# Attention and a gated unit on one core: K and Q in tiles of their own, small VectorE operations moved to ScalarE or PSUM

## The chip, the cores and the metric

The kernel runs on one core of a Trainium2 chip. The core has TensorE (PE in the profile; its weight loads are PEld), VectorE (DVE), ScalarE (ACT), GpSimd (POOL) and SyncE (SP), which here only issues the DMAs. Each engine works through a queue of its own in order; they meet through semaphores. SBUF is the working memory, PSUM holds TensorE's results in eight banks. The metric is the device time of one execution in microseconds; of the kernel before it is 1375.41 us, the median of 3 runs (1374.64 to 1376.36).

## The reference

Attention with queries that are averaged in pairs, and then a gated unit with a spatial product. All is float32 outside; two of the weights come as float64.

```python
# attention: B=8, H=8, S=1152, D=64
q_pool = q.reshape(B, H, S // 2, 2, D).mean(axis=3)          # 576 queries
scores = scale * np.matmul(q_pool, k.transpose(0, 1, 3, 2))  # 576 x 1152
attn = softmax(scores)                                       # with the row maximum taken away
x = (attn @ v) with the heads side by side                   # 8 x 576 x 512
# gated unit: w_in 512 x 1024, w_spatial 576 x 576, w_out 512 x 512
h = np.maximum(x @ w_in, 0.0)
u, v = h[..., :512], h[..., 512:]
v_n = (v - mean(v)) / np.sqrt(var(v) + 1e-06)
v_s = np.einsum('ts,bsd->btd', w_spatial, v_n) + b_spatial[None, :, None]
out = (u * v_s) @ w_out
```

## The kernel before

**Pairs and units.** The 64 heads are worked off as 32 pairs of one batch (`i` from 0 to 31). Two batches, so eight pairs, make one unit of the gated part; there are four units. Products are made with float16 or bfloat16 pieces of each operand, a high and a low part, so one float32 product is three matmuls.

**One pair.** `load_kq` (L218) fetches K and Q of the pair into one tile `kq`, K first, 576 KB each; the tile exists once. `prep` (L273) forms the squares' sums of K and Q on ScalarE (`square_sum`, L132), sums them over the partitions with a matmul of ones (L112), and makes of the sum's exponent a power of two for scaling, `s`, and its inverse, `r` (`scales`, L107: three VectorE operations L117, L121, L122 on a tile of two columns, with `h` = `qkh`, `s` = `qks`, `r` = `qkr`). The product of both `r` is `esc` (L287), the scale of the exponential. GpSimd adds Q's two halves (L292). Then the high parts come from ScalarE (L135 for Q, L302 and L304 for K) and the low parts from VectorE for Q (`rest`, L138) and from GpSimd for K (L305). Copies of halves across partitions go through DMAs (L299 to L313). `maxima` (L317) makes each query's maximum: 27 products per pair into `pm` banks and a maximum by VectorE for each (L348). `attention` (L498) makes the scores (L506, L507, bank `pss`), the exponential on ScalarE (L512, tile `pt`, and L520 for the tail), splits it on GpSimd (L524), and multiplies it with the values (L428, L432, L435, bank `o`).

**Beside the attention.** While pair `i` is worked on, `maxima` of pair `i + 1`, the values of the next ones (L229, L261 to L264) and `prep` of pair `i + 2` are mixed in at set rates, in the early pairs the decoding of the float64 weights (`from_double`, L144: masks, shifts and products on VectorE with L150 and L157 on ScalarE), and later a step of the gated unit (`gated_unit`, L546) at every second turn. In the unit, the first products give `vv` (L582, L590), statistics follow (L592, L593), four Newton steps for the inverse root (L611 to L614, on 9 columns), the normalised values (L618 to L624), the other half `u` (L646, L656), the spatial product (L688, L689, in two `pw` banks), bias and gate (L695 to L698), and the last product (L731). The last unit's later parts run after the last pair. The factors `r_h` (L568, L570), `r_v` (L635) and `r_y` (L707) are columns that scale a product back.

**What sets the order.** The source says what depends on what and in which order it is written; a scheduler then places the instructions in each engine's queue by its own estimate of when each can start, and adds the semaphores. So an edit at one place moves instructions at many others. PSUM is shared out by pools: 3 banks `pss`, 2 banks `pm` (maxima, the sums of `scales`, transposes), 1 bank `o`, 2 banks `pw` (the gated unit). A bank is given to the next user when the last instruction on its tile is done.

Of the kernel before, what the change touches and what calls it, by code (L numbers as in the profile page):

```python
# [12 lines left out]
F32 = mybir.dt.float32  # L13
I32 = mybir.dt.int32
I64 = mybir.dt.int64
AF = mybir.ActivationFunctionType
ALU = mybir.AluOpType
# [7 lines left out]
SVN = 2.0 ** 11  # L25
# [6 lines left out]
def attn_sgu_kernel(ctx: ExitStack, tc: tile.TileContext, qT, kT, v, w_in, w_spT, b_sp, w_out, out):  # L32
    nc = tc.nc
    P = 128
# [3 lines left out]
    KEYS = NC * P  # L38
# [67 lines left out]

    def scales(sq, name):  # L107


        n = sq.shape[1]  # L110
        pt = ps_m.tile([P, 512], F32, name="pm")
        nc.tensor.matmul(pt[:, :n], lhsT=ones, rhs=sq, start=True, stop=True)  # L112
        yield
        h = sm.tile([P, n], I32, name=name + "h", bufs=2)
        s = sm.tile([P, n], I32, name=name + "s", bufs=2)
        r = sm.tile([P, n], I32, name=name + "r", bufs=2)
        nc.vector.tensor_scalar(  # L117
            out=h, in0=pt[:, :n].bitcast(I32), scalar1=24, scalar2=0x7F, op0=ALU.logical_shift_right, op1=ALU.bitwise_and
        )
        c = float(2 ** 23)  # L120
        nc.vector.tensor_scalar(out=s, in0=h, scalar1=-c, scalar2=204 * c, op0=ALU.mult, op1=ALU.add)  # L121
        nc.vector.tensor_scalar(out=r, in0=h, scalar1=c, scalar2=50 * c, op0=ALU.mult, op1=ALU.add)  # L122
        return s.bitcast(F32), r.bitcast(F32)
# [7 lines left out]
    def square_sum(acc, src, junk):  # L131
        nc.scalar.activation(junk, src, AF.Square, bias=0.0, scale=1.0, accum_out=acc)  # L132

# [10 lines left out]
    def from_double(dst, src, t1, t2):  # L144


        V = nc.vector
        lo, hi = src[:, 0::2], src[:, 1::2]
        V.tensor_scalar(out=t1, in0=hi, scalar1=0xFFFFF, scalar2=None, op0=ALU.bitwise_and)
        nc.scalar.activation(dst, t1, AF.Copy, bias=1.0, scale=2.0 ** -20)  # L150
        V.tensor_scalar(out=t2, in0=lo, scalar1=1, scalar2=None, op0=ALU.logical_shift_right)
        yield
        V.scalar_tensor_tensor(out=dst, in0=t2, scalar=2.0 ** -51, in1=dst, op0=ALU.mult, op1=ALU.add)
        yield
# [9 lines left out]
    wsc = {}  # L164
# [53 lines left out]
    def load_kq(i):  # L218

        b, hp = divmod(i, NHP)  # L220
        kq = ld.tile([P, 2 * KEYS], F32, name="kq")
        nc.sync.dma_start(out=kq[:, 0:KEYS], in_=kT[b, hp].rearrange("h d c p -> (h d) (c p)"))
        nc.sync.dma_start(out=kq[:, KEYS:], in_=qT[b, hp].rearrange("h d r s -> (h d) (r s)"))
        state[i] = {"kq": kq}

# [47 lines left out]
    def prep(i):  # L273
        st = state[i]
        kq = st["kq"]
        X, KL, khh, qhl = (x[i % NSET] for x in (xq, klo, khi, qhi))
        k0 = kq[:, 0:KEYS].rearrange("p (c k) -> p c k", k=P)
        q0, q1 = kq[:, KEYS : KEYS + S], kq[:, KEYS + S :]
# [8 lines left out]
        nc.vector.scalar_tensor_tensor(  # L287
            out=esc, in0=r[:, 0:1], scalar=ESC, in1=r[:, 1:2], op0=ALU.mult, op1=ALU.mult
        )
        st["esc"] = esc  # L290
# [255 lines left out]
    def gated_unit(un):  # L546
# [20 lines left out]
        for e in range(2):  # L567
            nc.vector.tensor_mul(r_h[:, e : e + 1], vscale[2 * un + e][1], wsc["wi"])  # L568
# [40 lines left out]
        for k in range(4):  # L609
            z = SVN if k == 3 else 1.0  # L610
            nc.vector.tensor_mul(sd, rs, rs)  # L611
            nc.vector.tensor_mul(sd, sd, va)
            nc.vector.tensor_scalar(out=sd, in0=sd, scalar1=-0.5 * z, scalar2=1.5 * z, op0=ALU.mult, op1=ALU.add)
            nc.vector.tensor_mul(rs, rs, sd)  # L614
# [56 lines left out]
        def spatial(e, fc):  # L671
# [22 lines left out]
            for a, n, pz, ba in ((m0, MAIN, pv, 0), (tl0, TAIL, pvt, MAIN)):  # L694
                nc.vector.scalar_tensor_tensor(  # L695
                    out=gg[:, :n], in0=pz[:, :n], scalar=r_v, in1=b_bc[:, ba : ba + n], op0=ALU.mult, op1=ALU.add
                )
                nc.vector.tensor_mul(u[:, fc, a : a + n], u[:, fc, a : a + n], gg[:, :n])  # L698
            k = 2 * fc + e
# [3 lines left out]
        def split(n):  # L703
            a, z = groups[n]
            s_g, r_g = yield from scale_of(gsq[:, 2 * a : 2 * z], "g")
            r_y = sm.tile([P, 1], F32, name=f"r_y{n}")
            nc.vector.tensor_mul(r_y, r_g, wsc["wo"])  # L707
            if n == 0:
# [174 lines left out]
```

## Time and profile before

| | before |
|---|---|
| time, median of 3 runs | 1375.41 us (1374.64 to 1376.36) |
| the profiled execution | 1378.83 us, span 1377.1 us |
| mean granted TensorE clock | 0.967 |
| busy: TensorE, VectorE, ScalarE, GpSimd | 89%, 70%, 70%, 62% |
| bytes moved by DMAs | 123.77 MB |

A line of the groups is: source line, engine, operation, tiles written and read, shapes, count, then the busy time of the group in us with the mean of one in ns, and the idle time of the engine just before the group with what ended it. A line of the waits is: who waited, for whom, us in total, how often, the longest. A line of the windows is: from, to and length of the stretch, then for PE, PEld, DVE, ACT and POOL the busy time and the number of instructions, the granted clock, the DMA engines' share, GB/s; asked of one source line, it has that line's engine alone. A line of the order of time is: start, length, engine, line, operation, tiles, and in brackets the idle time before it. An instruction that has begun and waits inside the engine counts as busy.

### The profile page before, as it was taken

The numbers are of one execution on the slowest core, as the hardware profiler recorded it, in microseconds if no ns is written. First come the engines' busy times: TensorE is split into PE (matmuls) and PEld (weight loads), VectorE is DVE, ScalarE is ACT, GpSimd is POOL, SyncE is SP. The second block draws the span as 40 slices with busy tenths as digits, with TensorE's granted clock in tenths as the row PEclk, the third lists the DMA queues.
The fourth block names the chain that finished last, engine by engine and source line by source line (L and its number), as shares of the span: only waits on it lengthen the run. The fifth ranks groups of instructions, "written<-read, shape, count | busy, mean of one in ns | idle before, by whom it ended". The sixth has DMA issues, their size and how long they took to land.

```text
span 1377.1 us, 33478 instructions
## 1 busy us (share of the span) xinstructions
PE 1222.1 (89%) x13696; PEld 741.5 (54%) x13696; DVE 967.1 (70%) x2068; ACT 970.6 (70%) x1632; POOL 847.0 (62%) x492
## 2 busy tenths in 40 slices
PE   3677887788998999889998999889998999899998
PEld 1354555555554665556555666555555566556443
DVE  5799889986869767765668766775667866761455
ACT  6777678779966777768776886768776776655333
POOL 3587677878755666657774766667666576655000
PEclk9998899989999999999999999999999999999999
DMA  7533343434333231244332132244331131101002
GB/s 252 166 97 109 94 124 94 128 93 139 113 96 96 79 94 56 62 126 135 96 96 87 51 91 84 74 118 135 104 96 42 47 94 55 28 24 40 8 1 69
DMA packets 56346, 123.77 MB, mean 90 GB/s; under 512 B 8256, under 2 KB 16448, under 8 KB 56192
## 3 DMA queue, kind: packets, MB, share of 16 engines
q1 hardware_dynamic: 56192, 121.63, 29.8%
q8 instruction: 107, 1.75, 0.5%
q14 instruction: 47, 0.39, 0.1%
HBM read 83.56 MB, written 9.44 MB: 68 GB/s over the span
## 4 chain that ended last, share of the span: by engine, by line
PE 47%; DVE 25%; ACT 8%; POOL 7%; DMA 7%; issue 4%; SPq 1%; POOLq 0%; ACTq 0%; DVEq 0%
DVE mt L348 7%; PE pss L507 5%; PE pss L506 5%; PE pw L688 5%; POOL pt L524 4%; PE pm L342 4%; PE pw L731 4%; PE pw L646 3%; PE o L435 3%; PE o L428 3%; PE pw L582 3%; ACT pt L512 3%; DMA kq<-in_qT_dram 3%; PE o L432 3%; DVE vv L138 2%
## 5 line engine op out<-in xcount | busy, mean ns | idle before, releaser
L524 POOL TENSOR_TENSOR pt<-pt 128x1024 f16<-128x1024 f32 x288 | 567.8, 1977 | 265.9 <-ACT pt L512 253.8
L512 ACT ACTIVATE pt<-pss,lnp,esc 128x512 f32<-128x512 f32 x576 | 439.4, 776 | 156.7 <-PE pss L507 148.1
L348 DVE TENSOR_REDUCE mt<-pm 128x1 f32<-128x384 f32 x730 | 395.8, 552 | 139.1 <-PE pm L342 119.2
L435 PE MATMUL o<-vp,pt 128*128 128x65 f16 x2304 | 282.8, 198 | 20.2 <-POOL pt L524 19.9
L428 PE MATMUL o<-vp,pt 128*128 128x65 f16 x2304 | 284.8, 196 | 13.0 <-DVE xm L443 12.8
L506 PE MATMUL pss<-qhi,khi 128*128 128x64 f16 (+1 forms) x1152 | 279.6, 294 | 9.1 <-ACT pt L512 8.0
L432 PE MATMUL o<-vp,pt 128*128 128x64 f16 x2304 | 284.5, 196 | 0.0
L507 PE MATMUL pss<-xq,klo 66*128 66x64 f16 (+1 forms) x1152 | 280.6, 295 | 4.1 <-DMA xq<-mr 4.1
L428 PEld LDWEIGHTS <-pt 128*128 128x128 bf16 x2304 | 222.7, 101 | 85.1 <-DVE xm L443 22.0
L432 PEld LDWEIGHTS <-pt 128*128 128x128 bf16 x2304 | 221.6, 100 | 50.7 <-issue 10.5
L342 PE MATMUL pm<-khi,qhi 128*128 128x384 f16 x652 | 217.9, 335 | 32.6 <-DVE mt L348 27.7
L435 PEld LDWEIGHTS <-pt 128*128 128x128 f16 x2304 | 220.7, 100 | 31.6 <-POOL pt L524 24.8
L507 PEld LDWEIGHTS <-klo 66*128 66x128 f16 x1152 | 99.1, 100 | 48.8 <-issue 17.3
L132 ACT ACTIVATE klo<-kq 128x1152 f16<-128x1152 f32 x64 | 74.6, 1166 | 63.7 <-DMA kq<-in_kT_dram 49.4
L506 PEld LDWEIGHTS <-khi 128*128 128x128 f16 x1152 | 103.5, 100 | 27.9 <-issue 12.2
L342 PEld LDWEIGHTS <-qhi 128*128 128x128 f16 x768 | 76.8, 101 | 66.3 <-issue 28.5
L524 POOL TENSOR_TENSOR ptl<-ptl 128x1152 f16<-128x1152 f32 x32 | 71.1, 2221 | 57.9 <-ACT ptl L520 57.9
L305 POOL TENSOR_TENSOR klo<-kq,khi 128x640 f16<-128x640 f32 x64 | 85.1, 1341 | 20.1 <-ACT khi L304 19.8
L520 ACT ACTIVATE ptl<-pss,lnp,esc 128x256 f32<-128x256 f32 (+1 forms) x128 | 75.6, 591 | 24.8 <-PE pss L507 24.2
L264 POOL TENSOR_TENSOR vp<-vt,vp 128x576 f16<-128x576 f32 x64 | 80.6, 1264 | 20.3 <-ACT vp L262 20.3
L582 PE MATMUL pw<-wi_h,xg 128*128 128x512 f16 x240 | 90.1, 382 | 0.0
L731 PE MATMUL pw<-wo_h,vv 128*128 128x512 f16 x216 | 80.3, 381 | 4.7 <-DVE vv L138 4.7
(177 smaller groups left out, 2394.2 us busy)
## 6 DMA issues: line engine op xcount, KB each, us to landing
vt<-in_v_dram SPq DMA_DIRECT2D x64, 576.0 KB
kq<-in_kT_dram SPq DMA_DIRECT2D x32, 576.0 KB
kq<-in_qT_dram SPq DMA_DIRECT2D x32, 576.0 KB
khi<-khi SPq DMA_DIRECT2D x96, 144.0 KB
out_dram<-row SPq DMA_DIRECT2D x24, 256.0 KB
qhi<-xq SPq DMA_DIRECT2D x64, 72.0 KB
klo<-klo SPq DMA_DIRECT2D x32, 144.0 KB
vv<-in_w_in_dram SPq DMA_DIRECT2D x8, 512.0 KB
```

What stands on the lines that cost most here:

```text
L305: nc.gpsimd.tensor_sub(KL[:, 0, a:z], k0[:, a:z], khh[:, 1, a:z])
L342: nc.tensor.matmul(pm[:, :W], lhsT=qhl[:, h, c0 : c0 + P], rhs=khh[:, h, n * NB : (n + 1) * NB, :], start=True, stop=True,)
L348: nc.vector.reduce_max(out=mt[:, t, n : n + 1], in_=pm[:, :W], axis=AX.X)
L428: nc.tensor.matmul(o[:, t], lhsT=top[:, cols], rhs=vp[:, D : D + D1], start=c == 0 and t == 0, stop=False, skip_group_check=True,)
L432: nc.tensor.matmul(o[:, t, 0:D], lhsT=top[:, cols], rhs=vp[:, 0:D], start=False, stop=False, skip_group_check=True)
L435: nc.tensor.matmul(o[:, t], lhsT=rst[:, cols], rhs=vp[:, D : D + D1], start=False, stop=c == NC - 1, skip_group_check=True,)
L506: nc.tensor.matmul(o, lhsT=khh[:, h, c, :], rhs=qhl[:, h, q], start=True, stop=False)
L507: nc.tensor.matmul(o, lhsT=KL[0:KR, h, c, :], rhs=X[0:KR, h, q], start=False, stop=True)
L512: nc.scalar.activation(pt, ps, AF.Exp, bias=lnp, scale=esc)
L524: nc.gpsimd.tensor_sub(t.bitcast(F16)[:, :, 0::2], t, t.bitcast(BF16)[:, :, 1::2])
L582: nc.tensor.matmul(ph, lhsT=xa[:, cc, c0 : c0 + P], rhs=wa[:, cc, DH:DF], start=n == 0, stop=n == 3 * NCC - 1,)
L731: nc.tensor.matmul(py, lhsT=ga[:, fc, c0 : c0 + P], rhs=wa[:, fc, :], start=m == 0, stop=m == end - 1)
```

## The change

- K and Q get tiles of their own, `kt` (one buffer) and `qt` (two); Q is fetched first, and Q's sum of squares is formed before K's.
- `scales` keeps `h` in the PSUM bank of the sum, in columns beside it; `r` is made before `s`, and both have four buffers. The constant in `esc` moves into `r` for K and Q, as half its logarithm each.
- `esc`, `r_h`, `r_v` and `r_y` are made on ScalarE, as a copy with a column as scale; `r_h`'s third column comes straight from its factors, without the copy L570.
- `from_double` no longer shifts the low words by one bit (L151); the product L153 reads them as unsigned numbers with half the factor.
- In the Newton steps `va` and `sd` lie in a `pm` bank, and the products are formed in another order, so that each has one operand in PSUM and one in SBUF.
- The bias (L695) is written back to the `pw` bank, and the gate's product (L698) reads it there.

```diff
-    def scales(sq, name):
+    def scales(sq, name, up=0):
...
-        h = sm.tile([P, n], I32, name=name + "h", bufs=2)
-        s = sm.tile([P, n], I32, name=name + "s", bufs=2)
-        r = sm.tile([P, n], I32, name=name + "r", bufs=2)
+        h = pt[:, 16 : 16 + n].bitcast(I32)
+        s = sm.tile([P, n], I32, name=name + "s", bufs=4)
...
+        r = sm.tile([P, n], I32, name=name + "r", bufs=4)
+        nc.vector.tensor_scalar(out=r, in0=h, scalar1=c, scalar2=(50 + up) * c, op0=ALU.mult, op1=ALU.add)
         nc.vector.tensor_scalar(out=s, in0=h, scalar1=-c, scalar2=204 * c, op0=ALU.mult, op1=ALU.add)
-        nc.vector.tensor_scalar(out=r, in0=h, scalar1=c, scalar2=50 * c, op0=ALU.mult, op1=ALU.add)
...
-        lo, hi = src[:, 0::2], src[:, 1::2]
+        lo, hi = src.bitcast(U32)[:, 0::2], src[:, 1::2]
...
-        V.tensor_scalar(out=t2, in0=lo, scalar1=1, scalar2=None, op0=ALU.logical_shift_right)
-        yield
-        V.scalar_tensor_tensor(out=dst, in0=t2, scalar=2.0 ** -51, in1=dst, op0=ALU.mult, op1=ALU.add)
+        yield
+        V.scalar_tensor_tensor(out=dst, in0=lo, scalar=2.0 ** -52, in1=dst, op0=ALU.mult, op1=ALU.add)
...
-        kq = ld.tile([P, 2 * KEYS], F32, name="kq")
-        nc.sync.dma_start(out=kq[:, 0:KEYS], in_=kT[b, hp].rearrange("h d c p -> (h d) (c p)"))
-        nc.sync.dma_start(out=kq[:, KEYS:], in_=qT[b, hp].rearrange("h d r s -> (h d) (r s)"))
+        kt = ld.tile([P, KEYS], F32, name="kt")
+        qt = ld.tile([P, KEYS], F32, name="qt", bufs=2)
+        nc.sync.dma_start(out=qt, in_=qT[b, hp].rearrange("h d r s -> (h d) (r s)"))
+        nc.sync.dma_start(out=kt, in_=kT[b, hp].rearrange("h d c p -> (h d) (c p)"))
...
-        for j in range(2):
-            square_sum(sq[:, j : j + 1], kq[:, j * KEYS : (j + 1) * KEYS], KL[:, 0].rearrange("p c k -> p (c k)"))
+        for j, t in ((1, qt), (0, kt)):
+            square_sum(sq[:, j : j + 1], t, KL[:, 0].rearrange("p c k -> p (c k)"))
             yield
-        s, r = yield from scales(sq, "qk")
+        s, r = yield from scales(sq, "qk", math.log2(ESC) / 2)
         esc = sm.tile([P, 1], F32, name="esc", bufs=NSET)
-        nc.vector.scalar_tensor_tensor(
-            out=esc, in0=r[:, 0:1], scalar=ESC, in1=r[:, 1:2], op0=ALU.mult, op1=ALU.mult
-        )
+        nc.scalar.activation(esc, r[:, 0:1], AF.Copy, bias=0.0, scale=r[:, 1:2])
...
-            nc.vector.tensor_mul(r_h[:, e : e + 1], vscale[2 * un + e][1], wsc["wi"])
             rows = slice(e * TAIL, (e + 1) * TAIL)
-            nc.vector.tensor_copy(out=r_h[rows, 2:3], in_=r_h[rows, e : e + 1])
+            r_x = vscale[2 * un + e][1]
+            nc.scalar.activation(r_h[:, e : e + 1], r_x, AF.Copy, bias=0.0, scale=wsc["wi"])
+            nc.scalar.activation(r_h[rows, 2:3], r_x[rows], AF.Copy, bias=0.0, scale=wsc["wi"][rows])
...
-        va = sm.tile([P, NT], F32, name="va")
-        sd = sm.tile([P, NT], F32, name="sd")
+        pt = ps_m.tile([P, 512], F32, name="pm")
+        va, sd = (pt[:, 16 * k : 16 * k + NT] for k in range(2))
...
-            nc.vector.tensor_mul(sd, rs, rs)
-            nc.vector.tensor_mul(sd, sd, va)
+            nc.vector.tensor_mul(sd, rs, va)
+            nc.vector.tensor_mul(sd, rs, sd)
...
-        nc.vector.tensor_scalar_mul(r_v, wsc["ws"], 1.0 / SVN)
+        nc.scalar.activation(r_v, wsc["ws"], AF.Copy, bias=0.0, scale=1.0 / SVN)
...
-                    out=gg[:, :n], in0=pz[:, :n], scalar=r_v, in1=b_bc[:, ba : ba + n], op0=ALU.mult, op1=ALU.add
+                    out=pz[:, :n], in0=pz[:, :n], scalar=r_v, in1=b_bc[:, ba : ba + n], op0=ALU.mult, op1=ALU.add
                 )
-                nc.vector.tensor_mul(u[:, fc, a : a + n], u[:, fc, a : a + n], gg[:, :n])
+                nc.vector.tensor_mul(u[:, fc, a : a + n], u[:, fc, a : a + n], pz[:, :n])
...
-            nc.vector.tensor_mul(r_y, r_g, wsc["wo"])
+            nc.scalar.activation(r_y, r_g, AF.Copy, bias=0.0, scale=wsc["wo"])
```

The scheduler places the instructions anew, and the line numbers of the changed kernel are up to two higher. Three places of the queues follow. The first is SyncE's queue in one pair, in the stage with the gated unit; L222 and L223 fetch K and Q, L299 to L313 are the copies of `prep`, L363 those of the maxima, L741 stores the result. Before:

```order
L300 DMA qhi_120<-qhi_120 64x576
L307 DMA khi_117<-khi_117 64x1152
L308 DMA khi_117<-khi_117 64x1152
L309 DMA qhi_120<-xq_114 64x576
L312 DMA klo_108<-klo_108 64x1152
L222 DMA kq<-in_kT_dram 128x1152
L310 DMA khi_117<-khi_117 64x1152
L741 DMA out_dram<-row 128x512
L363 DMA xq_113<-mr 1x9x128 x2
L313 DMA klo_108<-klo_108 2x1152
L223 DMA kq<-in_qT_dram 128x1152
```

And of the changed kernel (L224 fetches Q, L225 fetches K):

```order
L300 DMA qhi_120<-qhi_120 64x576
L224 DMA qt<-in_qT_dram 128x1152
L309 DMA qhi_120<-xq_114 64x576
L307 DMA khi_117<-khi_117 64x1152
L308 DMA khi_117<-khi_117 64x1152
L312 DMA klo_108<-klo_108 64x1152
L225 DMA kt<-in_kT_dram 128x1152
```

K's fetch keeps its place behind the copy of K's low part (L312); Q's stood behind K's with four rows between, and stands ahead of it now with four rows between.

The second is VectorE's queue where the scales of a pair and of the first weight are made, in the early stage (`wih`, `wis`, `wir` are the weight's; L443 and L402 are the attention's output). Before:

```order
L117 TENSOR_SCALAR qkh<-pm 128x2
L117 TENSOR_SCALAR wih<-pm 128x1
L121 TENSOR_SCALAR qks<-qkh 128x2
L122 TENSOR_SCALAR qkr<-qkh 128x2
L121 TENSOR_SCALAR wis<-wih 128x1
L122 TENSOR_SCALAR wir<-wih 128x1
L287 SCALAR_TENSOR_TENSOR esc<-qkr 128x1
L348 TENSOR_REDUCE mt<-pw 128x1
L568 TENSOR_TENSOR r_h<-vr,wir 128x1 x2
L570 COPY r_h<-r_h 64x1 x2
L402 TENSOR_TENSOR xg<-pm,xg 128x512
```

And of the changed kernel:

```order
L118 TENSOR_SCALAR pm<-pm 128x2
L118 TENSOR_SCALAR pm<-pm 128x1
L151 TENSOR_SCALAR vv<-vv 128x512
L123 TENSOR_SCALAR qkr<-pm 128x2
L124 TENSOR_SCALAR qks<-pm 128x2
L123 TENSOR_SCALAR wir<-pm 128x1
L124 TENSOR_SCALAR wis<-pm 128x1
L402 TENSOR_TENSOR xg<-pm,xg 128x512
```

`esc` and `r_h` have left the queue, and the scales read the bank `pm`; a mask of the decoding (L151 there, L149 before) stands between.

The third is VectorE's queue at a gate of the first unit, between the maxima. Before:

```order
L695 SCALAR_TENSOR_TENSOR row<-pw,r_v,b_bc 128x512
L348 TENSOR_REDUCE mt<-pm 128x1 x2
L698 TENSOR_TENSOR u<-u,row 128x512
L348 TENSOR_REDUCE mt<-pm 128x1
L695 SCALAR_TENSOR_TENSOR row<-pw,r_v,b_bc 128x64
L348 TENSOR_REDUCE mt<-pm 128x1
L698 TENSOR_TENSOR u<-u,row 128x64
```

And of the changed kernel:

```order
L696 SCALAR_TENSOR_TENSOR pw<-pw,r_v,b_bc 128x512
L348 TENSOR_REDUCE mt<-pm 128x1 x3
L699 TENSOR_TENSOR u<-u,pw 128x512
L696 SCALAR_TENSOR_TENSOR pw<-pw,r_v,b_bc 128x64
L348 TENSOR_REDUCE mt<-pm 128x1
L699 TENSOR_TENSOR u<-u,pw 128x64
```

Three maxima stand between the bias and the gate now, and the bank `pw` is in use until the second of the two.

More of the change, by code (lines that the diff above doesn't have):

```diff
@@ L15 @@
 I64 = mybir.dt.int64
+U32 = mybir.dt.uint32
 AF = mybir.ActivationFunctionType
@@ L220, in load_kq @@
         b, hp = divmod(i, NHP)
-        kq = ld.tile([P, 2 * KEYS], F32, name="kq")
-        nc.sync.dma_start(out=kq[:, 0:KEYS], in_=kT[b, hp].rearrange("h d c p -> (h d) (c p)"))
-        nc.sync.dma_start(out=kq[:, KEYS:], in_=qT[b, hp].rearrange("h d r s -> (h d) (r s)"))
-        state[i] = {"kq": kq}
+        kt = ld.tile([P, KEYS], F32, name="kt")
+        qt = ld.tile([P, KEYS], F32, name="qt", bufs=2)
+        nc.sync.dma_start(out=qt, in_=qT[b, hp].rearrange("h d r s -> (h d) (r s)"))
+        nc.sync.dma_start(out=kt, in_=kT[b, hp].rearrange("h d c p -> (h d) (c p)"))
+        state[i] = {"kt": kt, "qt": qt}
     def load_v(i):
@@ L274, in prep @@
         st = state[i]
-        kq = st["kq"]
+        kt, qt = st["kt"], st["qt"]
         X, KL, khh, qhl = (x[i % NSET] for x in (xq, klo, khi, qhi))
-        k0 = kq[:, 0:KEYS].rearrange("p (c k) -> p c k", k=P)
-        q0, q1 = kq[:, KEYS : KEYS + S], kq[:, KEYS + S :]
+        k0 = kt.rearrange("p (c k) -> p c k", k=P)
+        q0, q1 = qt[:, 0:S], qt[:, S:]
         st.update(qhl=qhl, khh=khh, X=X, KL=KL)
         sq = sm.tile([P, 2], F32, name="sq", bufs=2)
-        for j in range(2):
-            square_sum(sq[:, j : j + 1], kq[:, j * KEYS : (j + 1) * KEYS], KL[:, 0].rearrange("p c k -> p (c k)"))
+        for j, t in ((1, qt), (0, kt)):
+            square_sum(sq[:, j : j + 1], t, KL[:, 0].rearrange("p c k -> p (c k)"))
             yield
-        s, r = yield from scales(sq, "qk")
+        s, r = yield from scales(sq, "qk", math.log2(ESC) / 2)
         esc = sm.tile([P, 1], F32, name="esc", bufs=NSET)
-        nc.vector.scalar_tensor_tensor(
-            out=esc, in0=r[:, 0:1], scalar=ESC, in1=r[:, 1:2], op0=ALU.mult, op1=ALU.mult
-        )
+        nc.scalar.activation(esc, r[:, 0:1], AF.Copy, bias=0.0, scale=r[:, 1:2])
         st["esc"] = esc
```

## The prediction

> **What bounds the kernel now.** I read the totals first, then the windows of the span, then VectorE's groups, then the waits and the order of single instructions at the places that these point to. The totals and four windows (length, busy time of PE, PEld, DVE, ACT, POOL, granted clock, DMA share, GB/s):
>
> ```profile
> PE 1222.1 (89%) x13696; PEld 741.5 (54%) x13696; DVE 967.1 (70%) x2068; ACT 970.6 (70%) x1632; POOL 847.0 (62%) x492
> 0.00:69.00 69.00, 34.20 (x227) 16.50 (x228) 45.77 (x98) 48.19 (x89) 30.90 (x29) 1.00 0.65 209
> 69.00:310.00 241.00, 191.49 (x2430) 126.26 (x2428) 213.82 (x389) 182.16 (x308) 183.34 (x102) 0.89 0.36 106
> 310.00:1240.00 930.00, 864.35 (x10053) 530.74 (x10052) 650.90 (x1449) 685.66 (x1141) 614.59 (x354) 0.98 0.29 86
> 1240.00:1378.00 138.00, 132.03 (x993) 67.95 (x991) 56.64 (x134) 54.63 (x96) 18.18 (x10) 0.99 0.09 30
> ```
>
> There are four stages. Up to 69 us the kernel starts, with loads of V on the chain that ended last (start, length):
>
> ```profile
> 20.93 6.80 DMA vt<-in_v_dram
> ```
>
> From 69 to 310 us, while the weights are decoded beside the attention, VectorE is busy 89% (213.8 of 241) and TensorE only 79%: VectorE sets the pace and TensorE stands still for 49.5 us. From 310 to 1240 us TensorE is busy 93% and stands still for 65.6 us; that is the most that any edit to another engine can win there. The tail is TensorE's, with 6 us to win.
>
> Where do the stops come from? VectorE's small operations show it: one operation, in a form of one column and one of two, and the same group's shortest, median and longest:
>
> ```profile
> L121 DVE TENSOR_SCALAR qks<-qkh 128x2 int32<-128x2 int32 x32 | 17.1, 533 | 0.6
> L121 DVE TENSOR_SCALAR qks<-qkh x32: 135/170/2074, 8.2 to 1170.8; 128x2 int32<-128x2 int32 x32
> L121 DVE TENSOR_SCALAR vs<-vh 128x1 int32<-128x1 int32 x8 | 1.2, 151 | 0.2
> L117 DVE TENSOR_SCALAR qkh<-pm 128x2 int32<-128x2 int32 x32 | 4.8, 150 | 16.4 <-PE pm L112 16.4
> ```
>
> The two-column form takes 170 ns at the median and up to 2074. The one-column form (151) and the two-column form that reads PSUM (150) show none of it. Now one long one, at 590 us, with what GpSimd and TensorE do:
>
> ```profile
> 590.20 1.90 POOL L524 TENSOR_TENSOR pt<-pt 128x1024 f16<-128x1024 f32 x1 [2.77 <-ACT pt L512]
> 590.26 1.86 DVE L121 TENSOR_SCALAR qks<-qkh 128x2 int32<-128x2 int32 x1
> 592.70 0.32 PE L342 MATMUL pm<-khi,qhi 128*128 128x384 f16 x1 [1.51 <-DVE mt L348]
> ```
>
> The small operation ends with GpSimd's (592.12 against 592.10): it waits for it while counting as busy. The row maxima L348 queue behind it on VectorE, and TensorE, which needs their bank, stops for 1.51 us.
>
> **The change part by part.** VectorE's groups that it removes or alters, and two that price the new forms:
>
> ```profile
> L287 DVE SCALAR_TENSOR_TENSOR esc<-qkr 128x1 f32<-128x1 f32 x32 | 16.8, 525 | 1.6
> L151 DVE TENSOR_SCALAR vv<-vv 128x512 int32<-128x512 int32 x12 | 14.2, 1184 | 0.1
> L568 DVE TENSOR_TENSOR r_h<-vr,wir 128x1 f32<-128x1 f32 x8 | 7.3, 951 | 14.0 <-ACT u L656 14.0
> L707 DVE TENSOR_TENSOR r_y<-gr,wor 128x1 f32<-128x1 f32 x5 | 4.7, 940 | 0.0
> L613 DVE TENSOR_SCALAR sd<-sd 128x9 f32<-128x9 f32 x16 | 7.5, 468 | 0.3
> L614 DVE TENSOR_TENSOR rs<-rs,sd 128x9 f32<-128x9 f32 x16 | 5.6, 351 | 0.3
> L698 DVE TENSOR_TENSOR u<-u,row 128x512 f32<-128x512 f32 x32 | 27.5, 858 | 0.4
> L698 DVE TENSOR_TENSOR u<-u,row 128x64 f32<-128x64 f32 x32 | 16.0, 499 | 0.4
> L402 DVE TENSOR_TENSOR xg<-pm,xg 128x512 f16<-128x512 f32 x32 | 21.8, 681 | 3.9 <-ACT xg L401 3.9
> L695 DVE SCALAR_TENSOR_TENSOR row<-pw,r_v,b_bc 128x64 f32<-128x64 f32 x27 | 7.5, 277 | 0.8
> ```
>
> Relief of VectorE:
> - Factors from PSUM: 17.1 becomes 32 x 0.150 = 4.8; saves 12.3.
> - esc goes to ScalarE: 16.8. r_h and r_y go too: 7.3 + 4.7 = 12.0.
> - The shift of the decoding (L151) goes: 14.2. L153 reads the low words with a step of two instead; I price that at nothing, since L151 read them so.
> - Newton steps (L613, L614) with an operand in PSUM: 13.1 becomes 32 x 0.150 = 4.8; saves 8.3.
> - Gate multiplications: 43.5 becomes 32 x 0.681 + 32 x 0.277 = 30.7; saves 12.8. [...]
>
> Sum: 12.3 + 16.8 + 12.0 + 14.2 + 8.3 + 12.8 = 76.4 us of 967. Some of it falls in the stage that VectorE bounds; the same window for L151, L287 and L121:
>
> ```profile
> 69.00:310.00 241.00, 10.94 (x8) 0.89 0.36 106
> 69.00:310.00 241.00, 8.94 (x6) 0.89 0.36 106
> 69.00:310.00 241.00, 7.33 (x9) 0.89 0.36 106
> ```
>
> That is 10.9 + 8.9 + (7.3 - 9 x 0.15) = 25.8. About 6 lie before 69 us, where the loads of V set the start: nothing won. The rest, about 45, lies between 310 and 1240.
>
> What of it reaches the end? From 69 to 310 between nothing and 25.8; VectorE is full to 89%, but GpSimd and ScalarE wait there too, so I take 15. From 310 on, TensorE is short of 65.6, of which this much stands as a direct wait for a maximum:
>
> ```profile
> PE pm L342 <- DVE mt L348: 20.1, 23, 2.2
> PE o L435 <- POOL pt L524: 19.9, 24, 2.3
> ```
>
> (The second row is of the whole span.) Bounds: nothing, and 45. I take 12, over half of the 20.1, since the one followed above, at 590 us, had a blocked small operation ahead of it.
>
> **K and Q.** One prep, at 666 us (SyncE's issues, ScalarE's two sums of squares, GpSimd's sum of Q's halves):
>
> ```profile
> 666.31 0.58 SPq L222 DMA_DIRECT2D kq<-in_kT_dram  x1
> 668.86 0.38 SPq L223 DMA_DIRECT2D kq<-in_qT_dram  x1
> 671.90 1.16 ACT L132 ACTIVATE klo<-kq 128x1152 f16<-128x1152 f32 x1 [3.53 <-DMA kq<-in_kT_dram]
> 674.91 1.16 ACT L132 ACTIVATE klo<-kq 128x1152 f16<-128x1152 f32 x1 [1.09 <-DMA kq<-in_qT_dram]
> 676.30 1.40 POOL L292 TENSOR_TENSOR kq<-kq 128x576 f32<-128x576 f32 x1 [5.89 <-ACT klo L132]
> POOL kq L292 <- ACT klo L132: 55.6, 12, 13.0
> ```
>
> Both loads wait until the pair before is split and its tile is free; Q comes second, and GpSimd stands at L292 with the splitting of the exponentials queued behind it. Now Q has a second buffer and is issued ahead of the copies that wait for K's split. K keeps its place, without Q's 576 KB beside it; the value loads behind it on SyncE stay where they were. L292 needs Q's square sum alone, so most of the 55.6 us of GpSimd's waits should go. TensorE's waits for GpSimd are 19.9 in all: between nothing and that, I take 3. In the start the second Q now passes weight pieces (576 KB at 209 GB/s, 2.8 us); these had no one waiting: nothing.
>
> **What it costs.** ScalarE gets 32 + 16 + 5 + 4 = 57 operations of one column. By the slope of these two:
>
> ```profile
> L656 ACT ACTIVATE u<-pw,r_h 128x512 f32<-128x512 f32 x28 | 19.2, 687 | 5.7 <-PE pw L646 5.5
> L656 ACT ACTIVATE u<-pw,r_h 128x64 f32<-128x64 f32 x28 | 7.2, 312 | 0.0
> ```
>
> (687 - 312) / 448 = 0.84 ns a column, so one column takes 0.26 us: 57 x 0.26 = 14.8 us on an engine that is 70% busy. esc waits for r, and the head of Q (L135) stands behind it; that waited for s anyway. Between nothing and 14.8 I take 2. Two kinds of PSUM bank are held longer. The Newton steps keep one of the two pm banks; and the gate:
>
> ```profile
> PE pw L689 <- DVE row L695: 1.2, 3, 0.5
> 494.28 0.75 DVE L695 SCALAR_TENSOR_TENSOR row<-pw,r_v,b_bc 128x512 f32<-128x512 f32 x1
> 495.31 0.38 PE L688 MATMUL pw<-ws_h,vv 128*128 128x512 f16 x1
> 495.46 0.68 DVE L698 TENSOR_TENSOR u<-u,row 128x512 f32<-128x512 f32 x1
> ```
>
> The next spatial block starts 0.28 us after L695 frees its bank; now the bank stays taken until L698 is done, at the earliest 0.7 us later. TensorE has attention in its queue meanwhile. Between nothing and 21 starts x 2.4 (the later ends, with three maxima of 0.55 between), I take 3, Newton included.
>
> Sum: 15 + 12 + 3 - 2 - 3 = 25 us. The profiled execution took 1378.8 us (span 1377.1); 25 less is 1353.8. It was 3.4 above the median of the runs shown, so I predict **1350 us** against 1375.4.
>
> [...]
>
> **The rivals.**
> - The relief passes on whole (1321 us): 25.8 early, 25 of the 45 later, 8 by K and Q, less 5, is 54. For it: VectorE's 89%, and a granted clock of 0.89 early against 0.98 later, where TensorE is fuller. Against: GpSimd and ScalarE are at 76% there.
> - The waits move (1366 us): other VectorE operations that read SBUF twice, such as L138, still meet GpSimd, and the stop appears there. Early 6, late 5, less 2, is 9.
> - Slower: the gate's banks. TensorE's queue is in order; if it stands at each of 21 starts (seven in each of three units) until L698 has ended, this decides from 25 / 21 = 1.2 us each, and at 1.7 each the time is 1350 + 36 = 1386. For it: the 0.28 us in the last fence. Against: only 1.2 us of such waits now (that fence's first row), and the order moves these starts.
> - It does not do what it says: PSUM forms wait for GpSimd as well, 1375 us. Against: L117.
>
> **How the numbers follow.** Forecast 0.45 (own range 1338 to 1362), whole relief 0.20, moved waits 0.23, gate banks 0.08, no effect 0.04. The range 1322 to 1370 leaves out the last two and a part of the whole relief's own spread. 0.2% (2.75 us) is about what a measurement tells from no change. Faster: 0.45 + 0.20 + 0.21 = 0.86; same 0.04 + 0.02 = 0.06; slower 0.08.
>
> **What would show it.** In the profile of the changed kernel: the factors' operations near 150 ns with no long ones; VectorE's busy time near 890 us; the stage up to 310 us shorter by about 15; TensorE's stops after it near 55 us; GpSimd's wait at the sum of Q under 20. Wrong, if TensorE waits at the first product of a spatial block, or if L138 grows by what the small ones lost.

## The result, and the profile after

The changed kernel takes **1332.3 us** (median of 4 runs, 1329.41 to 1340.43) against 1375.03 us before (4 runs, 1374.26 to 1376.36). The ratio is 0.9698, with a 95% interval of 0.9654 to 0.9741. The forecast was 1350, its range 1322 to 1370. The direction and the range held; the gain was 43 us where 25 were forecast. The profiled execution of the changed kernel took 1332.94 us (span 1330.8, mean granted clock 0.974), so it stands 0.6 above its median, where that of before stood 3.4 above. So some 3 us of the difference between the two profiles below come from a profiled execution of before that was longer than its median.

The totals and the four windows of the changed kernel, in the columns of the prediction's first fence:

```profile
PE 1205.3 (91%) x13696; PEld 736.8 (55%) x13696; DVE 914.8 (69%) x1999; ACT 979.2 (74%) x1689; POOL 845.4 (64%) x492
0.00:69.00 69.00, 37.25 (x284) 18.71 (x285) 45.26 (x101) 51.48 (x96) 36.91 (x33) 1.00 0.71 224
69.00:310.00 241.00, 198.41 (x2610) 132.80 (x2607) 217.59 (x399) 198.56 (x342) 198.70 (x110) 0.91 0.39 114
310.00:1240.00 930.00, 882.56 (x10285) 543.74 (x10282) 605.81 (x1392) 696.28 (x1188) 609.78 (x352) 0.99 0.29 84
1240.00:1331.00 91.00, 87.06 (x530) 41.54 (x527) 46.15 (x108) 32.84 (x65) 0.00 (x0) 1.00 0.08 27
```

VectorE works 52.3 us less (967.1 before), not 76.4 less. TensorE is busy 16.8 us less with the same 13696 matmuls, in part a matter of its clock, below. From 310 to 1240 us it stands still for 47.4 us instead of 65.6.

Windows at fixed times compare different work once one kernel is ahead. So the next table is worked out from the trace, between the starts of the split of the scores' tail (GpSimd, L524, tile `ptl`) in pairs 0, 8, 16, 24 and 31. The stops leave out the time ahead of TensorE's first matmul and behind its last. "Clock" is the most that a halved granted clock can have cost: half the length of the stretches where it was 0.5. TensorE itself stood still for 10.4 us of these stretches before and 4.8 after, so the column counts a part of the stops again.

| stage | length before, after (us) | shorter by | TensorE's stops before, after | clock before, after |
|---|---|---|---|---|
| start to pair 0 | 57.9, 52.9 | 5.0 | 26.4, 22.2 | 0, 0 |
| pair 0 to 8 (decoding) | 277.3, 262.0 | 15.3 | 54.3, 44.8 | 29.0, 22.2 |
| pair 8 to 16 | 321.7, 311.5 | 10.2 | 23.2, 17.2 | 6.8, 5.1 |
| pair 16 to 24 | 316.4, 306.6 | 9.8 | 20.8, 15.4 | 5.1, 3.4 |
| pair 24 to 31 | 273.4, 267.5 | 5.9 | 17.9, 13.7 | 3.4, 3.4 |
| pair 31 to the end | 130.4, 130.2 | 0.2 | 1.3, 1.1 | 0.4, 0.1 |

Of the 46.4 us, 29.5 are fewer stops and at most 10.5 less time at half clock (about 8 without the stops inside those stretches); the other 6 to 9 are busy time of TensorE that I can't divide further.

VectorE's groups of the changed kernel, which answer to the rows of the second and fourth fences (the old L121, L151, L153, L161 and L618 are now L124, gone, L154, L162 and L619):

```profile
L124 DVE TENSOR_SCALAR qks<-pm x32: 137/150/152, 8.3 to 1129.9; 128x2 int32<-128x2 int32 x32
L614 DVE TENSOR_SCALAR pm<-pm 128x9 f32<-128x9 f32 x16 | 2.7, 169 | 0.2
L615 DVE TENSOR_TENSOR rs<-rs,pm 128x9 f32<-128x9 f32 x16 | 2.6, 164 | 0.3
L699 DVE TENSOR_TENSOR u<-u,pw 128x512 f32<-128x512 f32 x27 | 18.3, 678 | 0.0
L151 DVE TENSOR_SCALAR vv<-vv 128x512 int32<-128x512 int32 x12 | 15.8, 1319 | 0.9 <-DMA vv<-in_w_in_dram 0.9
L154 DVE SCALAR_TENSOR_TENSOR u<-vv,u 128x512 f32<-128x512 uint32 x12 | 19.7, 1639 | 2.0 <-ACT u L152 1.9
L162 DVE TENSOR_TENSOR u<-u,vv 128x512 f32<-128x512 f32 x12 | 19.8, 1652 | 0.1
L619 DVE TENSOR_SCALAR row<-vv,mv,rs x36: 539/547/2112, 392.5 to 1267.4; 128x512 f32<-128x512 f32 x36
```

The first row is shortest, median, longest: no factor operation is long any more, 152 ns at most. The Newton steps and the gate read near their forecast prices. But the decoding that was left has become slower. Of before, the same groups:

```profile
L149 DVE TENSOR_SCALAR vv<-vv 128x512 int32<-128x512 int32 x12 | 10.0, 833 | 1.5 <-DMA vv<-in_w_in_dram 1.5
L153 DVE SCALAR_TENSOR_TENSOR u<-vv,u 128x512 f32<-128x512 int32 x12 | 12.3, 1026 | 2.0 <-ACT u L150 1.8
L161 DVE TENSOR_TENSOR u<-u,vv 128x512 f32<-128x512 f32 x12 | 17.7, 1474 | 0.1
```

These three took 40.0 us and now take 55.3. With the shift and the two other groups of the decoding, it took 82.9 us before and takes 84.7 after, though one of its six groups is gone. That the product waits is seen in its ends: the eleven of L154 that took over 700 ns all end 544 to 549 ns behind the end of an instruction of GpSimd, while its shortest took 671 ns, where the old L153 had 674.

The waits of the changed kernel, and one row of before that answers to the third:

```profile
PE pm L342 <- DVE mt L348: 17.3, 23, 1.9
PE o L435 <- POOL pt L524: 19.6, 22, 2.1
PE pm L333 <- DVE xg L402: 19.4, 9, 2.9
POOL qt L292 <- ACT klo L134: 10.6, 12, 2.5
PE pw L690 <- ACT u L657: 5.1, 3, 2.2
```

```profile
PE pm L333 <- DVE xg L402: 10.8, 4, 3.6
```

The stops behind a maximum fell from 27.7 to 17.3 (the prediction's 20.1 was its part between 310 and 1240). Those behind `xg` rose from 10.8 to 19.4. One of these in order of time, in pair 10 of the changed kernel:

```profile
392.19 2.11 POOL L524 TENSOR_TENSOR ptl<-ptl 128x1152 f16<-128x1152 f32 x1 [0.84 <-ACT ptl L520]
392.50 4.11 DVE L619 TENSOR_SCALAR row<-vv,mv,rs 128x512 f32<-128x512 f32 x2
394.10 0.38 PE L507 MATMUL pss<-xq,klo 66*128 66x512 f16 x1
394.25 2.08 POOL L524 TENSOR_TENSOR pt<-pt 128x1024 f16<-128x1024 f32 x1
397.40 0.68 DVE L402 TENSOR_TENSOR xg<-pm,xg 128x512 f16<-128x512 f32 x1
398.13 0.35 PE L333 MATMUL pm<-khi,qhi 128*64 128x384 f16 x2 [2.92 <-DVE xg L402]
399.14 0.63 PE L507 MATMUL pss<-xq,klo 66*128 66x512 f16 x1
```

Two normalising operations (L619), which take 0.54 us when free, take 4.11 together, because GpSimd splits exponentials from 392.19 to 396.33 (each of the two ends 0.28 us behind one of GpSimd's). L402 and with it the `pm` bank come late, and TensorE stops for 2.92 us. Then it pays again: the same matmul takes 0.38 us before the stop and 0.63 just after it. The windows of the changed kernel before and across this stop, the third figure from the end of a row being the granted clock:

```profile
385.00:395.00 10.00, 10.00 (x125) 6.49 (x122) 9.21 (x33) 6.50 (x12) 5.89 (x4) 1.00 0.20 61
395.00:405.00 10.00, 7.08 (x60) 3.49 (x59) 8.27 (x16) 7.32 (x15) 3.23 (x2) 0.83 0.21 70
```

Half the matmuls of the 10 us before are done. In the whole trace of before the clock is halved 17 times, for 3.4 or 6.8 us; 11 of the 17 begin during or within 2 us behind a stop of over 1.8 us, the others behind one to three shorter ones.

### The profile page after: what moved, and what is told of

It reads as the page before. It is cut to its first block, busy times and chain, and to the rows that moved or that the text cites. A ratio compares the mean times of both kernels' runs of the same rounds, so it can differ in the third digit from the quotient of the medians.

```text
span 1330.8 us, 33477 instructions
## 1 busy us (share of the span) xinstructions
PE 1205.3 (91%) x13696; PEld 736.8 (55%) x13696; DVE 914.8 (69%) x1999; ACT 979.2 (74%) x1689; POOL 845.4 (64%) x492
## 4 chain that ended last, share of the span: by engine, by line
PE 58%; DVE 16%; POOL 8%; ACT 8%; issue 5%; DMA 5%; SPq 1%; POOLq 0%; ACTq 0%; DVEq 0%
PE pss L507 7%; PE pss L506 7%; PE pm L342 6%; PE pw L732 5%; PE pw L689 5%; POOL pt L524 5%; DVE mt L348 5%; PE pw L583 5%; PE o L435 4%; PE o L428 3%; PE o L432 3%; PE pw L647 3%; DMA vt<-in_v_dram 3%; DVE vv L140 2%; ACT pt L512 2%
## 5 line engine op out<-in xcount | busy, mean ns | idle before, releaser
L524 POOL TENSOR_TENSOR pt<-pt 128x1024 f16<-128x1024 f32 x288 | 563.7, 1962 | 259.6 <-ACT pt L512 252.8
L435 PE MATMUL o<-vp,pt 128*128 128x65 f16 x2304 | 283.2, 198 | 19.6 <-POOL pt L524 19.6
L428 PEld LDWEIGHTS <-pt 128*128 128x128 bf16 x2304 | 222.9, 101 | 76.1 <-issue 19.4
L342 PE MATMUL pm<-khi,qhi 128*128 128x384 f16 x652 | 216.9, 334 | 19.6 <-DVE mt L348 17.3
L524 POOL TENSOR_TENSOR ptl<-ptl 128x1152 f16<-128x1152 f32 x32 | 69.7, 2178 | 51.9 <-ACT ptl L520 51.9
L266 POOL TENSOR_TENSOR vp<-vt,vp 128x576 f16<-128x576 f32 x64 | 83.4, 1308 | 30.1 <-ACT vp L264 30.1
L305 POOL TENSOR_TENSOR klo<-kt,khi 128x640 f16<-128x640 f32 x64 | 85.8, 1347 | 24.3 <-ACT khi L304 24.3
L647 PE MATMUL pw<-xg,wi_h 128*128 128x512 f16 (+1 forms) x336 | 81.4, 329 | 0.2 <-ACT u L657 0.2
```

The costliest lines, as they stand in the source:

```text
L342: nc.tensor.matmul(pm[:, :W], lhsT=qhl[:, h, c0 : c0 + P], rhs=khh[:, h, n * NB : (n + 1) * NB, :], start=True, stop=True,)
L428: nc.tensor.matmul(o[:, t], lhsT=top[:, cols], rhs=vp[:, D : D + D1], start=c == 0 and t == 0, stop=False, skip_group_check=True,)
L435: nc.tensor.matmul(o[:, t], lhsT=rst[:, cols], rhs=vp[:, D : D + D1], start=False, stop=c == NC - 1, skip_group_check=True,)
L524: nc.gpsimd.tensor_sub(t.bitcast(F16)[:, :, 0::2], t, t.bitcast(BF16)[:, :, 1::2])
L647: nc.tensor.matmul(pu[:, : z - a], lhsT=wa[:, cc, fc * P : (fc + 1) * P], rhs=xa[:, cc, a:z], start=n == 0, stop=n == 3 * NCC - 1,)
```

## The experiments

The theory was that of the prediction: VectorE's operations that read SBUF twice, or in a form of two columns or more, wait for GpSimd while they count as busy (in the kernel before, L121 up to 2074 ns where its median is 170); each one freed shortens the queue before the maxima, and so TensorE's stops. The rivals: the gate's banks cost what the gate gains; K and Q carry more than was forecast; and the waits move to those operations that still read SBUF. All kernels below compute the whole reference. Each ratio is against the kernel before on the same chip. It is formed from all the runs and can differ by about a thousandth from the quotient of the two medians; what a run won or lost in us goes by the ratio.

**The factors alone.** `h` in PSUM, `r` made before `s`, `esc` on ScalarE, on the kernel before.

```diff
-        h = sm.tile([P, n], I32, name=name + "h", bufs=2)
...
+        h = pt[:, 16 : 16 + n].bitcast(I32)
...
-        nc.vector.scalar_tensor_tensor(out=esc, in0=r[:, 0:1], scalar=ESC, in1=r[:, 1:2], ...)
+        nc.scalar.activation(esc, r[:, 0:1], AF.Copy, bias=0.0, scale=r[:, 1:2])
```

> The kernel before with the factors alone (h in PSUM, r before s, esc on ScalarE). Relief of VectorE 12.3 + 16.8 = 29 us of the 76. Theory W: 10 to 18 us less, 1357 to 1365 us. Theory L: under 8 us, 1367 us or more. If relief counts by its size alone, 29/76 of the 35 that W gives to VectorE, 13 us.

Measured: 1360.61 us against 1371.18, ratio 0.9913 (0.9884 to 0.9943), so 12 us for 29 us of VectorE's time.

**The gate alone.** The bias back into the bank, the product reads it there.

```diff
-    out=gg[:, :n], in0=pz[:, :n], scalar=r_v, ...
+    out=pz[:, :n], in0=pz[:, :n], scalar=r_v, ...
...
-    nc.vector.tensor_mul(u[...], u[...], gg[:, :n])
+    nc.vector.tensor_mul(u[...], u[...], pz[:, :n])
```

> The kernel before with the gate alone (bias written back to the bank pw, product read from there). Relief 12.8 us, all after 490 us. Theory W: 2 to 6 us less, 1369 to 1373 us. The rival of the banks: each of 21 spatial blocks starts 0.7 to 2.4 us later and TensorE stands for it, 1380 us or more, with waits of TensorE for the gate's product; if TensorE has other work, no such waits.

Measured: 1364.96 us, ratio 0.9942 (0.992 to 0.9963): 8 us won, more than was expected. The rival of the gate's banks falls.

**The decoding alone.** Without the shift.

```diff
-        lo, hi = src[:, 0::2], src[:, 1::2]
+        lo, hi = src.bitcast(U32)[:, 0::2], src[:, 1::2]
...
-        V.tensor_scalar(out=t2, in0=lo, scalar1=1, scalar2=None, op0=ALU.logical_shift_right)
...
-        V.scalar_tensor_tensor(out=dst, in0=t2, scalar=2.0 ** -51, in1=dst, op0=ALU.mult, op1=ALU.add)
...
+        V.scalar_tensor_tensor(out=dst, in0=lo, scalar=2.0 ** -52, in1=dst, op0=ALU.mult, op1=ALU.add)
```

> The kernel before with the decoding alone (no shift of the low words). Relief 14.2 us, 10.9 of it between 69 and 310 us, where VectorE is 89% busy. Theory W: 5 to 11 us less (ratio 0.992 to 0.996), won before 310 us and nothing after 400. Theory L or S (the order that the scheduler makes decides, not the relief): any size, not bound to the stage.

Measured: 1367.42 us against 1370.72, ratio 0.9971 (0.996 to 0.9983), so 4 us, a little less than was expected.

**Newton steps and columns.** `va` and `sd` in a `pm` bank, with the products in their new order; `r_h`, `r_v` and `r_y` on ScalarE.

```diff
-        va = sm.tile([P, NT], F32, name="va")
-        sd = sm.tile([P, NT], F32, name="sd")
+        pt = ps_m.tile([P, 512], F32, name="pm")
+        va, sd = (pt[:, 16 * k : 16 * k + NT] for k in range(2))
...
-            nc.vector.tensor_mul(r_y, r_g, wsc["wo"])
+            nc.scalar.activation(r_y, r_g, AF.Copy, bias=0.0, scale=wsc["wo"])
```

> The kernel before with the Newton steps in PSUM and r_h, r_v, r_y on ScalarE. Relief 8.3 + 12.0 us, nearly all after 190 us, in the four units. Theory W, with the parts adding up to the 34 us of all parts but K and Q (12 and 8 have been measured): 14 less those of the decoding, so 4 to 10 us (ratio 0.993 to 0.997). If the pm bank kept by Newton costs what is won: no change.

Measured: 1372.99 us against 1370.72, ratio 1.0012 (0.9993 to 1.0032): nothing, for some 20 us of VectorE's time by the forecast.

**K and Q alone, and all but K and Q.** The first is the kernel before with `kt` and `qt`, the second the changed kernel with `kq`.

```diff
-        kq = ld.tile([P, 2 * KEYS], F32, name="kq")
...
+        kt = ld.tile([P, KEYS], F32, name="kt")
+        qt = ld.tile([P, KEYS], F32, name="qt", bufs=2)
...
```

> The kernel before with the K and Q part alone (tiles of their own, Q first, two buffers; all small operations as before). Theory W (the gain is VectorE no longer waiting for GpSimd, and the loads give the start and a little): 4 to 8 us less, 1367 to 1371 us, GpSimd's wait at the sum of Q gone, VectorE's long small operations still there. Theory L (the loads are the larger part of the 43 us, since the stage after 310 us won 27 where 12 were given to VectorE's relief): 20 us less or more, 1355 us or under.

> The changed kernel with the K and Q part undone. Theory W: 33 to 39 us less than before, 1336 to 1342 us; VectorE's busy time near 915 us. Theory L: 10 to 22 us less, 1353 to 1365 us. Together with the run of K and Q alone: if the two gains add to 43, the parts are independent; if they add to clearly less, each needs the other.

Measured: K and Q alone 1370.77 us against 1371.18, ratio 0.9985 (0.996 to 1.0011); all but K and Q 1338.57, ratio 0.9752 (0.9728 to 0.9776). Against the whole change's 0.9698 that leaves half a per cent, some 7 us, for K and Q on top of the rest, where alone they gave some 2 (0.9985, an interval that takes in no change). The intervals 0.9728 to 0.9776 and 0.9654 to 0.9741 nearly meet, so the 7 are uncertain. The waits show both. K and Q alone:

```profile
PE o L436 <- POOL pt L525: 14.3, 20, 2.2
PE pw L343 <- DVE mt L349: 16.8, 19, 1.7
```

And all but K and Q:

```profile
POOL kq L290 <- ACT klo L133: 34.1, 16, 13.5
PE o L433 <- POOL pt L522: 30.7, 30, 2.5
```

Alone, they took 5.6 us from TensorE's wait for GpSimd (19.9 before), and 10 came back in the waits for maxima in `pw` banks (6.8 before). In all, TensorE stood still for 152.9 us of the span instead of 155.0. In the changed kernel they cut 30.7 to 19.6. That it reads like the 19.9 of before is chance: the other edits together had raised it to 30.7, and K and Q brought it back.

**One column at a time.** Does the wait hang on the form or on PSUM? On the kernel before, `s` and `r` of K and Q are formed by two operations of one column each, still from SBUF.

```diff
-        nc.vector.tensor_scalar(out=s, in0=h, scalar1=-c, ...)
+        for j in range(n):
+            m = slice(j, j + 1)
+            nc.vector.tensor_scalar(out=s[:, m], in0=h[:, m], scalar1=-c, ...)
...
```

> The kernel before with each of the operations for s and r done as two of one column, in SBUF, nothing in PSUM; one look, for the durations. [...] Time: within 4 us of the kernel before.

Its groups, in shortest, median and longest:

```profile
L123 DVE TENSOR_SCALAR qks<-qkh x64: 120/144/155, 8.2 to 1159.0; 128x1 int32<-128x1 int32 x64
L289 DVE SCALAR_TENSOR_TENSOR esc<-qkr x32: 141/302/1539, 8.5 to 1159.3; 128x1 f32<-128x1 f32 x32
```

The long ones are gone without PSUM (155 against 2074 ns), while `esc`, which takes two columns from SBUF as two operands, keeps them (1539). So the form decides in these rows; why it does isn't shown. A single run took 1367.24 us, against a median of 1370.72 before; one run shows no difference in time.

**Where the wait goes.** The kernel of the Newton steps and columns, and the normalised rows in a `pm` bank besides, so that L618 and L624 no longer wait for GpSimd either (on the mean 922 and 1008 ns before, 806 and 689 in this run).

```diff
-            vn = wk.tile([P, DH], F32, name="row")
+            vn = ps_m.tile([P, 512], F32, name="pm")
```

> The kernel before with the Newton steps and the columns r_h, r_v, r_y as in the change (alone: ratio 1.001), and the normalised rows in a bank pm as in the run before (on top of the change: 0.992). Theory B (alone, the relief was eaten since the normalisation then comes as one block, its 72 operations wait for GpSimd, and TensorE stops there and loses clock): with these operations freed the whole is clearly more than the second part, ratio 0.984 to 0.990. Rival (Newton's hold on a pm bank costs what its relief wins): only the second part is seen, ratio 0.991 to 0.996.

Measured: 1379.67 us against 1370.63, ratio 1.0067 (1.0045 to 1.0089). More VectorE work was freed, and the kernel is slower than before, which neither side had expected. Its factors, still in SBUF, say where a part of the wait went; they took 533 and 525 ns before:

```profile
L121 DVE TENSOR_SCALAR qks<-qkh 128x2 int32<-128x2 int32 x32 | 24.2, 756 | 0.7
L287 DVE SCALAR_TENSOR_TENSOR esc<-qkr 128x1 f32<-128x1 f32 x32 | 24.1, 752 | 1.8 <-DVE qkr L122 0.5
```

That is 14 us more for the two groups. I read it so: with the freed operations done sooner, these arrive while GpSimd is at work more often. So I asked what happens if the factors are freed on top of it, with the diff of the first experiment.

> The run of Newton steps, columns and normalised rows in PSUM, without the factors' part, was slower than before (1.0067); in its trace the factors' operations on SBUF (L121, L287) waited 7 us more each. This kernel adds the factors' part alone (h in the PSUM bank, esc on ScalarE), which alone gave 0.9913. Theory A, the wait for GpSimd moves from the freed operations to those that still read SBUF twice, and the loss was that: with the factors freed too, the gain is more than the product of the two, 1.0067 x 0.9913 = 0.998: between 0.970 and 0.988, and the stops of TensorE in the stage up to the split of pair 8 fall below 50 us. Theory B, the loss has another cause (a pm bank held for the normalised rows, or the order), so the two multiply: 0.994 to 1.002.

Measured: 1352.51 us against 1372.3, ratio 0.985 (0.9833 to 0.9866), within the range of theory A and outside that of B. Its stops from pair 0 to 8 were 52.0 us, 2 above what A had set, so A's second sign failed; most of the gain lies behind pair 8, where the stops were 63.2 in the kernel before, 66.1 in the run without the factors, and are 47.6 here. The same edit, the factors', is worth 0.9% on the kernel before and 2.2% here (0.985 by 1.0067).

**The Newton steps taken back.** The changed kernel with `va` and `sd` in SBUF, as before.

> The changed kernel (ratio 0.970) with the Newton steps alone put back into SBUF, in their old order. If Newton in PSUM is worth a part of its 8.3 us of relief: 2 to 6 us slower, ratio 0.971 to 0.975, and long operations of up to 1.8 us among the steps again. If the bank held for Newton costs more than the relief: 0.970 or less.

Measured: 1342.7 us, ratio 0.9795 (0.976 to 0.9831): within the change the Newton steps in PSUM are worth about 1%, though with the columns they gave nothing on the kernel before. That is more than their 7.7 us of VectorE's time. It lies beyond both expectations. Its stops behind a maximum are 25.0 us instead of 17.3. Those behind `xg` are 10.6 instead of 19.4: the changed kernel has three of 2.9 us (the one shown above in pair 10, and one each in pairs 18 and 26) that this run doesn't have. So the Newton steps in PSUM brought these stops and won more elsewhere.

**A better version: what still waits.** First the normalised rows in a `pm` bank, now on the changed kernel, so that L619 and L625 (on the mean 994 and 1020 ns in the changed kernel) no longer wait for GpSimd.

> The changed kernel, and the normalised rows also in a bank pm (written by L619, read by ScalarE and by L625), so that these 72 operations of 512 columns have one operand in SBUF. Theory W: L619 from 994 to near 700 ns and L625 from 1020 to near 690, relief 23 us in the stages of the units where TensorE still stops for 5 to 7 us: 4 to 10 us less than the changed kernel, ratio to the kernel before 0.962 to 0.967. Rival: each row holds one of the two pm banks for 3 us, maxima go through the other, and it is no faster than the changed kernel (0.970) or slower.

Measured: 1318.71 us against 1370.72, ratio 0.9624 (0.9594 to 0.9653). The edit that went with a loss when the factors still read SBUF wins some 10 us here. Its L619 (shortest, median, longest) and L625:

```profile
L619 DVE TENSOR_SCALAR pm<-vv,mv,rs x36: 792/806/816, 391.9 to 1254.0; 128x512 f32<-128x512 f32 x36
L625 DVE TENSOR_TENSOR vv<-pm,vv 128x512 f16<-128x512 f32 x36 | 24.8, 689 | 9.6 <-ACT vv L624 9.0
```

L619 is dearer than I had expected. Its median is 259 ns longer than in the changed kernel (547), the longest 1.3 us shorter. In the pairs where rows are normalised the long ones counted for more: the stops of pair 26 fell from 7.4 to 0.4 us, those of pairs 10 and 18 from 5.6 to 4.0 and from 5.7 to 3.9.

Then the decoding's temporaries in the two `pw` banks as well, with the maxima of the early pairs on `pm` banks alone.

```diff
+        t1 = ps_w.tile([P, 512], F32, name="pw").bitcast(I32)
+        m = ps_w.tile([P, 512], F32, name="pw")
...
-        V.tensor_mul(dst, dst, t2.bitcast(F32))
+        V.tensor_mul(dst, m, t2.bitcast(F32))
...
-                if units or (t + n) % 2:
+                if True:
```

> The changed kernel, the normalised rows in a bank pm (0.962), and the decoding's two temporaries in the two pw banks, so that none of its operations has more than one operand in SBUF or writes SBUF from SBUF but the last; the maxima then use the pm banks alone from the start. Theory W: the decoding's operations from 1319, 1639, 1182, 1268 and 1652 ns to 700 to 850, relief about 39 us, nearly all before 310 us: 8 to 18 us less than 0.962, ratio 0.949 to 0.956. Rival: with two banks in place of four for the maxima TensorE and VectorE wait for each other before 310 us, ratio 0.962 or more.

Measured: **1304.72 us** against 1370.63, ratio 0.952 (0.9494 to 0.9546), the fastest of all. One group of its decoding (the old L154, 1639 ns) and its window from 69 to 310 us:

```profile
L156 DVE SCALAR_TENSOR_TENSOR pw<-vv,pw 128x512 f32<-128x512 uint32 x12 | 8.3, 689 | 3.8 <-ACT pw L154 3.8
69.00:310.00 241.00, 211.51 (x2840) 139.83 (x2839) 194.29 (x443) 215.69 (x377) 206.69 (x119) 0.98 0.42 127
```

VectorE is off its limit there (194.3 of 241 instead of 217.6) and the granted clock is 0.98 instead of 0.91. The start to pair 0 became longer, 60.8 us instead of 52.9; nothing was tried on that, and the two edits, banks for the decoding and fewer for the maxima, were not run apart.

## Why the prediction was right, and where its sizes were not

The bound was read rightly: from 69 to 310 us VectorE, later TensorE with stops whose cause, in the two that were followed (1.51 us in the kernel before, 2.92 in the changed one), is GpSimd. The five signs, one by one:

- **Factors near 150 ns with no long ones**: right, 148 and 153 ns, the longest 160.
- **VectorE near 890 us**: wrong, 914.8. Of the relief of 76.4 us, the factors (12.4), `esc` (16.8), the columns (12.0) and the Newton steps (7.7) came as forecast, and the gate gave a little more (14.9, less 0.5 on the bias). The decoding's 14.2 did not: the group total rose by 1.8, so that term was off by 16. The prediction's step "I price that at nothing, since L151 read them so" looked at the access, and the access costs little: alone, the edit took 11.5 us off the decoding (82.9 to 71.4). In company the remaining operations, which read SBUF twice or in a form of many columns, wait longer (the three groups above take 55.3 us instead of 40.0). The normalised rows (3.0 more) and the low parts of the weights (6.2 more) did the same. So the prediction's sign of being wrong, that L138 grows by what the small ones lost, came in part: it grew by 7.2 us (95.6 to 102.8, L140 now), where factors, `esc`, columns and Newton steps lost 49.
- **The stage to 310 shorter by about 15**: 15.3 between the splits of pairs 0 and 8. The size is right, but it can't be claimed to 1 us: that stage's clock loss alone lay between 13.7 and 29.0 us from one of the kernels above to another (the fastest left out), and the profile of before had the highest.
- **Stops after it near 55 us**: 47.4 between 310 and 1240. This is the term that was mis-sized. "I take 12, over half of the 20.1" for the late relief and 3 for K and Q, less 5 of costs, is 10; the stages behind pair 8 became 26.1 us shorter. Three things were missing. The 20.1 counts only what stands as a direct wait for a maximum; waits for `xm` (12.8 to 6.7) fell too, while those for GpSimd's split stayed (19.9 to 19.6) and those for `xg` rose (10.8 to 19.4). Many stops had a second price, the half clock behind them (at most 45 us in the kernel before, 34 in the changed one). And the parts do more together than alone: the five single runs multiply to 0.982, 24 us, the whole gives 0.970, 41 us on the same chips' 1371.
- **GpSimd's wait at the sum of Q under 20 us**: right, 10.6, though nearly half of the fall from 55.6 came without the K and Q part (34.1). The step behind it, "TensorE's waits for GpSimd are 19.9 in all: between nothing and that, I take 3", was near what K and Q gave alone (some 2) and low by about 4 on top of the rest (7).

The start was forecast at nothing and gave 5.0 us. No run singles out the cause: without K and Q it is 54.8, with the factors alone 56.2, with K and Q alone 57.2, by one profile each.

The costs: ScalarE's new operations took 16.3 us (9.4 for `esc` at 293 ns each) where 14.8 were estimated; what of it reaches the end wasn't singled out. The gate's banks cost nothing that shows: no row of the waits names L696 or L699 for TensorE, and the spatial products wait for ScalarE alone (5.1).

The time lies below the likeliest case's own range (1338 to 1362), between the forecast 1350 and the rival "the relief passes on whole" (1321), and nearer to the rival. But that rival's sum fits no better: of its 25.8 early the stage won 15, and its 25 late and 8 by K and Q stand against 26 for both. "The waits move" was seen at work, in the decoding, in L619 and at `xg`, without deciding the sign; in the run of Newton steps, columns and rows it did decide it. "Slower by the gate's banks" and "no effect" fell. An operand in PSUM cost little on small operations: the two-column forms that read it (L124 and L123 of the changed kernel) have medians of 150 and 159 ns, the one-column form in SBUF 144, so 6 to 15 ns less.

What stays open: why the moved wait cost the run with 1.0067 more than it had won. Its factors' 14 us are shown, and that freeing them turns the loss into a gain; the path from them to TensorE's stops was not followed one by one. Every edit also gives the queues a new order, and no run changes the order alone; what it adds to the single gains isn't known.

## What to carry to other kernels

An operation that waits inside its engine counts as busy in these profiles (the L121 of 1.86 us at 590.26 of the kernel before, where the median is 0.17), so read shortest, median and longest of a group, and take the median of the free form as its price. Free all operations on the path that can meet the other engine: single ones gave less than their time here (the factors 12 us for 29), and one choice of them made the kernel slower (1.0067), while the wait of the next that can meet it grew (by 14 us). Price a stop of TensorE at its length and, where half clock follows, at what that costs (here at most half of 3.4 to 10.2 us each time).

## What the runs showed of the hardware

- The granted clock was halved for 3.4 or 6.8 us at a time in both kernels, once for 10.2 us in the changed one, behind stops of which most are shorter than 3.4 us. A matmul of the kernel before, with the stop ahead of it in brackets:

```profile
416.82 0.32 PE L342 MATMUL pm<-khi,qhi 128*128 128x384 f16 x1 [2.19 <-DVE mt L348]
```

And the window with it, where the granted clock was 0.66 on the mean (half of full from 417.0 for 6.8 us):

```profile
415.00:425.00 10.00, 7.90 (x63) 4.67 (x63) 8.15 (x27) 4.64 (x9) 3.07 (x2) 0.66 0.28 75
```

Series of stops near 1 us stand ahead of it too (1.03 us at 130.2 and 0.83 at 132.9; half clock from 133.7). But not every such stop is followed by it: one of 2.39 us at 1197.3 of the kernel before and one of 2.91 at 1011.5 of the changed kernel had none. In all, half clock cost at most 45 us of the kernel before, 34 of the changed one, and 12 of the fastest (half of the time at half clock).
- A normalising operation of 128x512 took 539 ns at its shortest and 547 at the median from SBUF to SBUF (the changed kernel's L619), and 806 at the median into PSUM (the same line with the rows in a `pm` bank); the first reached 2112 with the wait, the second never passed 816.
